# Gated linear attention and a gated SSM on one core: an opening in chunks, a later load of w_out, and other places for the steps of turns 1 to 5

## The chip, the core and the metric

The kernel runs on one core of a Trainium2 chip. The core has five engines with queues of their own, each of which works strictly in order: PE (TensorE, matrix products into PSUM), DVE (VectorE), ACT (ScalarE), POOL (GpSimd) and SP (SyncE, which here only issues DMAs). They meet through semaphores. The metric is the time of the whole program on the device in microseconds. A profiled execution gives, beside that time, the span and every instruction in it.

## The reference

Two blocks follow each other. All inputs are float32, save the weights of the second, which come as float64 and are cut to float32 bits on the chip.

```python
# attention: B, H, S, D = 4, 8, 768, 48; alpha lies between 0.8 and 1
for t in range(S):
    state = alpha[:, :, t, :, None] * state + einsum('bhd,bhe->bhde', k[:, :, t], v[:, :, t])
    y[:, :, t] = einsum('bhd,bhde->bhe', q[:, :, t], state)
x = y with the heads side by side                  # (4, 768, 384)
# gated SSM: w_in is 384 x 1024, w_out 512 x 384
val, gate = split(x @ w_in)
h = exp(A_log)[0] * h + val[:, t]                  # a scan over t, for 512 channels
out = (silu(gate) * h) @ w_out                     # (4, 768, 384)
```

## The kernel before

The sequence is cut into twelve turns of 256 steps, three to a batch element. A turn `m` passes through these stages, each a function of the program.

- Loads (`load_steps`, `load_raw`, `load_v`): alpha, q and k come with time over the partitions and must be turned so that the head's 48 channels lie over partitions. For turns 0 to 2 (and alpha of 3) PE turns them by products with the identity (`turned`) and ACT copies them out of PSUM; from turn 3 on DVE turns them with a stream transpose (`turn`). One buffer a name holds the raw steps, so a load waits until the turn before has been turned. Loads are issued by SP, one after the other.
- `scan_P` and `scan_V`: DVE's two scans of 1028 elements, the running product of alpha forwards and its sum backwards. `scaled_k` and `scaled_q` multiply k and q by them into `Zk` and `Zq`.
- `scores` (PE) and `masks` (DVE, ACT, POOL), together `first`: products of `Zk` and `Zq`, masked into `A` and `AK`. From turn 3 on the mask of `AK` is POOL's (line 762).
- `values(m, True)`, `states` and `add_up`, together `second`: masked scores times v, the states of four blocks of 64 steps, and their running sums `sum` on POOL (lines 828 and 830), or on DVE (`add_banks`) for the first batch element.
- `carried`, `values(m, False)` and `join`, together `third`: the part of the output that comes from earlier states, and the bringing of the two halves of y into `xT`, by ACT and by eight small DMAs.
- `project(n, cc)` for four pieces `cc`: 6 products with a piece of w_in, three for `val` and three for `gate`, then DVE's scan `hh` over `val` (line 932), ACT's `sg` = silu of `gate`, and their product, on DVE in the turns 0, 1 and 11 and on POOL in the others (line 942). `output(n)`: 8 products with w_out, ACT's eviction and the store.

The schedule is written out by hand: the order of the calls is the order of each engine's queue. Turn `n` of the loop projects turn `n` and does the attention of turn `m = n + 1`. DVE's seven steps for the turn after (turn alpha, scan P, turn k, scan V, `Zk`, turn q, `Zq`) are a generator, `products`, and `go(count)` takes the next `count` of its steps. Four PSUM banks (`ps_mm`) go round among turned pieces, scores, projections and outputs; the scores and y have four of their own.

w_in comes in pieces of 128 columns for each of `val` and `gate`. `low(i)` has ACT convert the low bits of piece `i`, `convert(i)` does the high bits on DVE (lines 553 and 555) and the sum on POOL (line 557); pieces 4 and 5 are w_out.

The opening, before the loop, is turn 0: turned alpha of turn 0 in four banks (line 694), q and k, alpha of turn 1, the scans, scores, masks, `first_values`, `states`, `first_states`, `first_carried` and `first_join`, with turning and converting for turn 1 in between. A memset of one element of the raw alpha by POOL (line 1001) holds back SP's loads behind it until w_in 0 is converted.

Of the kernel before, what the change touches and what calls it, by code (L numbers as in the profile page):

```python
# [346 lines left out]
def fast(  # L347
# [41 lines left out]
    p2 = pool("p2", 2)  # L389
    ps_at = pool("ps_at", 1, space=PS)  # L390
# [56 lines left out]
    units = [range(0, 1), range(1, 2), range(2, 4)]  # L447
# [45 lines left out]
    def constants():  # L493
# [18 lines left out]
        for t in dS[0] + dS[1]:  # L512
            nc.vector.memset(t[:, :, :, D:64], 0.0)
        for t in sums:
            nc.vector.memset(t[:, :, D:64], 0.0)
        nc.vector.memset(K0[:, :, :, D:], 0.0)
# [22 lines left out]
    def low(i):  # L539
        bits, w = bits_of(i)  # L540
        r = p2.tile([C, UW], I32, tag="wr", name="wr")
        lows[i] = r.rearrange("p (a n) -> p a n", a=w.shape[1])
        halves = lows[i].bitcast(U16).rearrange("p a (n two) -> p a n two", two=2)
        nc.scalar.activation(halves[:, :, :, 0], bits[:, :, :, 0], AF.Copy, scale=2.0 ** -29)

    def convert(i):
        if i not in lows:
            low(i)
        bits, w = bits_of(i)
        r = lows.pop(i)  # L550
        halves = r.bitcast(U16).rearrange("p a (n two) -> p a n two", two=2)
        quarters = bits.rearrange("p a n two -> p a (n two)").bitcast(U16).rearrange("p a (n four) -> p a n four", four=4)
        nc.vector.tensor_scalar(out=w.bitcast(U32), in0=bits[:, :, :, 1], scalar1=3, scalar2=0x3FFFFFFF,
                                op0=ALU.logical_shift_left, op1=ALU.bitwise_and)
        nc.vector.tensor_scalar(out=halves[:, :, :, 1], in0=quarters[:, :, :, 3], scalar1=0xC000, scalar2=None,  # L555
                                op0=ALU.bitwise_and)
        nc.gpsimd.tensor_tensor(out=w.bitcast(I32), in0=w.bitcast(I32), in1=r, op=ALU.add)  # L557
# [126 lines left out]
    def turned(m, name, js, t):  # L684
        raw = steps_of(name, m)
        tp = t[:, 0:len(js) * C].rearrange("p (j x) -> p j x", j=len(js))
        if (m, name) in ((1, "k"), (1, "q"), (3, "a")):
# [10 lines left out]
    def copy_turned(to, js, tp, engine=None):  # L698
        place = by_runs(to)[:, :, :, js.start:js.stop]
        if engine:  # L700
            return engine.tensor_copy(out=place, in_=tp)
        return nc.scalar.activation(place, tp, AF.Copy)

    def turn_over(m, name, to, tags=(None, None)):
        size = NJ // len(tags)
        copies = []
        for n, tag in enumerate(tags):
            js = range(size * n, size * (n + 1))
            copy = copy_turned(to, js, turned(m, name, js, bank(tag)), nc.vector if n % 2 and tag else None)
            if tag:  # L710
                for other in copies[(n + 1) % 2::2]:
                    tc.declare_no_dep(copy.ins, other.ins, reason="the copies write different steps")
                copies.append(copy)

    def alphas(m, tags=(None, None)):
        turn_over(m, "a", by_place(als[m % 2])[:, :, 1:GP], tags)
# [31 lines left out]
    def masks(m):  # L748
        sc = [[t[:, 0:4 * (L + D)].rearrange("p (h x) -> p h x", h=4) for t in pair] for pair in scs.pop(m)]
        mb = mask[:, None, :]  # L750
        if m < NG:
            for c in range(G):
# [162 lines left out]
    def project(n, cc, late=False):  # L915
# [10 lines left out]
        for vg, kk in order:  # L926
            nc.tensor.matmul((pv, pg)[vg], w_ins[cc][:, kk, vg, :], xT[:, kk, :],  # L927
                             start=(kk == 0), stop=(kk == NK - 1))
# [67 lines left out]
    for js, part in zip(halves, parts):  # L996
        copy_turned(tk, js, part)
# [230 lines left out]
```

## Time and profile before

| what | us |
|---|---|
| median of 3 runs | 278.73 (278.04 to 279.35) |
| the profiled execution | 279.43 |
| its span | 277.7 |
| PE busy in the span | 268.8 (97%) |
| DVE busy | 218.3 (79%) |
| POOL busy | 122.4 (44%) |
| ACT busy | 108.6 (39%) |
| first product with w_in starts at | 23.39 |

The clock that the throttle granted TensorE is 1.00 throughout. Times of the profile count from the start of the span. The chain that ended last lists, in order of time, the start of a piece, its length, and the engine, tile and line (or "issue", where an engine waited for nothing that the profile shows). A float32 product appears as two records. The instructions in order of time carry the start, the length, the engine, line and operation, output and input tiles, and in brackets the idle time just before and what ended it. A row of waits gives who waited, for whom, the sum, the count and the longest.

### The profile page before, as it was taken

The numbers are of one execution on the slowest core, as the hardware profiler recorded it, in microseconds if no ns is written. First come the engines' busy times: TensorE is split into PE (matmuls) and PEld (weight loads), VectorE is DVE, ScalarE is ACT, GpSimd is POOL, SyncE is SP. The second block draws the span as 40 slices with busy tenths as digits, with TensorE's granted clock in tenths as the row PEclk, the third lists the DMA queues.
The fourth block names the chain that finished last, engine by engine and source line by source line (L and its number), as shares of the span: only waits on it lengthen the run. The fifth ranks groups of instructions, "written<-read, shape, count | busy, mean of one in ns | idle before, by whom it ended". The sixth has DMA issues, their size and how long they took to land.

```text
span 277.7 us, 9598 instructions
## 1 busy us (share of the span) xinstructions
PE 268.8 (97%) x4056; PEld 217.0 (78%) x4056; DVE 218.3 (79%) x281; ACT 108.6 (39%) x244; POOL 122.4 (44%) x141
## 2 busy tenths in 40 slices
PE   7999999999989999899999999999999999999995
PEld 5988887876678688488688688688688688787874
DVE  7979998898798995995895995996995993079540
ACT  2577763461332532341542433433434425213111
POOL 8141223130068574563473584484384476435000
PEclk9999999999999999999999999999999999999999
DMA  6949993845919777487468587576687501201201
GB/s 196 295 140 309 296 262 78 205 88 139 267 48 238 149 199 182 103 214 163 103 181 199 114 205 164 130 197 155 152 186 159 144 0 27 77 1 33 71 5 59
DMA packets 51599, 41.18 MB, mean 148 GB/s; under 512 B 27360, under 2 KB 49536, under 8 KB 51552
## 3 DMA queue, kind: packets, MB, share of 16 engines
q1 hardware_dynamic: 48752, 37.50, 53.1%
q0 software_dynamic: 1408, 2.03, 2.8%
q10 hardware_dynamic: 1392, 0.99, 1.2%
q8 instruction: 33, 0.54, 0.9%
q14 instruction: 14, 0.11, 0.2%
HBM read 32.54 MB, written 4.72 MB: 134 GB/s over the span
## 4 chain that ended last, share of the span: by engine, by line
PE 92%; DVE 3%; DMA 1%; POOL 1%; issue 1%; ACT 1%; SPq 0%; DVEq 0%; ACTq 0%
PE mm L927 45%; PE mm L956 21%; PE y L791 4%; PE y L778 4%; PE mm L744 3%; PE s L744 3%; PE s L810 3%; PE mm L694 2%; PE mm L1189 2%; DMA raw_a<-in_alpha_dram 1%; POOL AK L762 1%; DVE P L630 1%; DVE V L649 1%; PE mm L689 1%; PE y L862 1%
## 5 line engine op out<-in xcount | busy, mean ns | idle before, releaser
L927 PE MATMUL mm<-xT,w_in 128*128 128x256 f32 x576 | 128.9, 382 | 0.6 <-ACT xT L884 0.6
L927 PEld LDWEIGHTS mm<-xT,w_in 128*128 128x128 f32 x576 | 108.1, 190 | 16.3 <-issue 0.8
L956 PE MATMUL mm<-w_out,f_last 128*128 128x384 f32 x160 | 54.1, 492 | 1.3 <-DVE A L759 1.3
L940 ACT ACTIVATE sg<-mm 128x256 f32<-128x256 f32 x48 | 18.4, 384 | 85.8 <-PE mm L927 80.3
L956 PEld LDWEIGHTS mm<-w_out,f_last 128*128 128x128 f32 x160 | 29.7, 190 | 21.1 <-issue 1.4
L830 POOL TENSOR_TENSOR sum<-sum,dS 128x192 f32<-128x192 f32 x30 | 33.2, 1108 | 27.3 <-PE mm L927 13.5
L942 POOL TENSOR_TENSOR f_last<-sg,hh 128x256 f32<-128x256 f32 x36 | 30.9, 862 | 30.6 <-ACT sg L940 23.1
L932 DVE TENSOR_TENSOR_SCAN hh<-a_dec,hh,mm 128x256 f32<-128x256 f32 x32 | 23.4, 732 | 15.4 <-PE mm L927 15.2
L630 DVE TENSOR_TENSOR_SCAN P<-al,lower 128x1028 f32<-128x1028 f32 x12 | 31.1, 2595 | 0.6
L649 DVE TENSOR_TENSOR_SCAN V<-al,ends 128x1028 f32<-128x1028 f32 x12 | 28.3, 2356 | 0.4
L907 POOL DMA_DIRECT2D xT<-yst x40 | 20.5, 517 | 13.1 <-ACT yst L904 11.8
L950 ACT ACTIVATE o_sb<-mm 128x384 f32<-128x384 f32 x22 | 10.8, 491 | 38.4 <-PE mm L956 38.4
L762 POOL TENSOR_TENSOR AK<-AK,mask 128x512 f32<-128x512 f32 x9 | 13.2, 1464 | 17.2 <-ACT AK L760 17.2
L759 DVE TENSOR_TENSOR A<-s,mask 128x256 f32<-128x256 f32 x9 | 3.8, 425 | 21.5 <-PE s L744 21.5
L557 POOL TENSOR_TENSOR w_in<-w_in,wr 128x768 int32<-128x768 int32 x4 | 7.3, 1826 | 26.0 <-DVE wr L555 17.0
L595 DVE STREAM_TRANSPOSE k<-raw_k 128x1024 f32<-128x1024 f32 x9 | 18.3, 2033 | 0.0
L595 DVE STREAM_TRANSPOSE q<-raw_q 128x1024 f32<-128x1024 f32 x9 | 18.2, 2022 | 0.0
L778 PEld LDWEIGHTS y<-AK,v 64*64 64x64 f32 x352 | 12.1, 134 | 6.4 <-issue 5.0
L595 DVE STREAM_TRANSPOSE al<-raw_a 128x1024 f32<-128x1024 f32 x8 | 16.3, 2041 | 0.1
L778 PE MATMUL y<-AK,v 64*64 64x64 f32 x352 | 14.5, 221 | 1.0 <-POOL AK L762 1.0
L791 PEld LDWEIGHTS y<-Zq,sum 48*64 48x64 f32 x656 | 11.8, 134 | 4.3 <-issue 4.1
L791 PE MATMUL y<-Zq,sum 48*64 48x64 f32 x656 | 14.4, 221 | 0.6 <-issue 0.6
(158 smaller groups left out, 392.2 us busy)
## 6 DMA issues: line engine op xcount, KB each, us to landing
v<-in_v_dram SPq DMA_DIRECT2D x22, 192.0 KB, 3.3
out_dram<-o_sb SPq DMA_DIRECT2D x22, 192.0 KB, 2.1
raw_k<-in_k_dram SPq DMA_DIRECT2D x18, 184.0 KB, 3.4
raw_q<-in_q_dram SPq DMA_DIRECT2D x18, 184.0 KB, 3.8
raw_k<-in_k_dram SPq DMA_DIRECT2D x18, 176.0 KB, 3.8
raw_q<-in_q_dram SPq DMA_DIRECT2D x18, 176.0 KB, 4.1
raw_a<-in_alpha_dram SPq DMA_DIRECT2D x16, 184.0 KB, 5.0
raw_a<-in_alpha_dram SPq DMA_DIRECT2D x16, 176.0 KB, 5.1
```

The costliest lines, as they stand in the source:

```text
L595: nc.vector.transpose(out=by_runs(to).rearrange("p h c j -> p h j c"), in_=raws[name][:, 0:4 * ROW].rearrange("p (h j d) -> p h j d", h=4, ...
L630: nc.vector.tensor_tensor_scan(out=P, data0=al[:, 0:4 * GP], data1=lower.rearrange("p h t -> p (h t)"), initial=0.0, op0=ALU.mult, op1=ALU ...
L649: nc.vector.tensor_tensor_scan(out=V[:, ::-1], data0=al[:, 1:4 * GP + 1][:, ::-1], data1=ends.rearrange("p h t -> p (h t)")[:, ::-1], init ...
L778: nc.tensor.matmul(ys[m][i][ds(64 * s, 64), e, ds(c * C + h * L, L)], v_sb[rows, c, 4 * i + p, :], As[i][rows, c, p, :], start=across and ...
L791: nc.tensor.matmul(ys[m][i][ds(64 * s, 64), e, ds(u * L, L)], Ss[j][rows, p, :], Zqs[m % 2][rows, u, p, D:], start=False, stop=True, skip_ ...
L830: nc.gpsimd.tensor_add(Ss[j][:, :, 0:D], Ss[j - 1][:, :, 0:D], part)
L907: engines[n % len(engines)].dma_start(out=xT[to, a], in_=st[rows, i, e])
L927: nc.tensor.matmul((pv, pg)[vg], w_ins[cc][:, kk, vg, :], xT[:, kk, :], start=(kk == 0), stop=(kk == NK - 1))
L932: nc.vector.tensor_tensor_scan(out=hh, data0=a_dec[:, cc:cc + 1].to_broadcast([C, GC]), data1=pv, initial=prev_h[cc][:, GC - 1:GC] if n % ...
L940: nc.scalar.activation(sg, pg, AF.Silu)
L942: f = lambda: engine.tensor_mul(fs[n][cc], sg, hh)
L956: nc.tensor.matmul(os[c], fs[n][cc][:, ds(c * C, C)], w_outs[cc // 2][:, cc % 2, :], start=(cc == 0), stop=(cc == NI - 1))
```

## The change

The opening works in smaller chunks: alpha of turn 0 is turned in quarters of 64 x 64 (`first_alphas`), q with its second half first (`first_q`), and k of turn 0 and alpha of turn 1 by transposes. The turned halves of k and q of turn 1 stand one by one between the scores, the states and the join. The masks of turn 0 come ahead of the conversion of w_in 0, and the conversion of w_in 1 moves behind the V scan of turn 1. Memsets of padding leave DVE: those of `dS` and `K0` fall away, those of `sums` are written by ACT. An ACT write after the first states takes the place of the memset that held back the loads.

In turn 0 the turning of alpha of turn 2 goes ahead of projection (0,1); the gate products of (0,0) and (0,1) go to turn 1, with four buffers for `sg`; values and states of turn 1 go between the two halves of projection (0,2). The load of w_out goes from the end of the opening to behind the third step of turn 1, and the load of k of turn 3 behind w_out. The last pieces of w_in are loaded one by one.

Later, `second(3)` and `second(5)` move behind the second projection of their turn, `first(5)` behind the output of turn 3, and `go` calls are moved so that three of DVE's steps for turn 6 fall into turn 3. The k of turn 4 is loaded behind the moves of the join, and the join of turn 2 uses both queues. From turn 5 on the order of PE, DVE, ACT and POOL is as before.

```diff
+    gates = pool("gates", 4)
...
-    units = [range(0, 1), range(1, 2), range(2, 4)]
+    units = [range(i, i + 1) for i in range(NI)]
...
-        for t in dS[0] + dS[1]:
-            nc.vector.memset(t[:, :, :, D:64], 0.0)
-        for t in sums:
-            nc.vector.memset(t[:, :, D:64], 0.0)
-        nc.vector.memset(K0[:, :, :, D:], 0.0)
...
     def convert(i):
         if i not in lows:
             low(i)
...
+        high(i)
+        add_low(i)
...
+    turned_by_transpose = ((0, "k"), (1, "a"), (1, "k"), (1, "q"), (3, "a"))
...
+    def first_alphas():
+        raw, to = steps_of("a", 0), by_runs(by_place(als[0])[:, :, 1:GP])
+        tps = [[bank(tag)[:, 0:NJ // 2 * 64].rearrange("p (j x) -> p j x", x=64) for tag in tags]
+               for tags in (("s0", "s1"), ("y1", "y0"))]
+        def turn_quarter(j, i, r):
+            rows = ds(64 * r, 64)
+            nc.tensor.matmul(tps[j // 4][r][ds(64 * i, 64), j % 4], raw[rows, ds(i * ROW + j * D, 64)],
+                             ident[rows, rows], start=True, stop=True, skip_group_check=True)
+        for j in range(2):
+            for r in range(2):
+                turn_quarter(j, 1, r)
+        for j in range(NJ):
+            for r in range(2):
+                turn_quarter(j, 0, r)
+                if j + 2 < NJ:
+                    turn_quarter(j + 2, 1, 1 - r)
...
+        for n in range(2):
+            for r in range(2):
+                place = to[:, :, ds(16 * r, 16), 4 * n:4 * n + 4]
+                part = tps[n][r].rearrange("p j (c h) -> p h c j", h=4)
+                copy = nc.vector.tensor_copy(out=place, in_=part) if r else \
+                    nc.scalar.activation(place, part, AF.Copy)
...
+    def first_q():
+        raw, to = steps_of("q", 0), plain("q")
+        tps = [bank().rearrange("p (j x) -> p j x", x=C) for _ in halves]
+        def turn_half(j, i):
+            nc.tensor.matmul(tps[j // 4][ds(64 * i, 64), j % 4], raw[:, ds(i * ROW + j * D, 64)], ident,
+                             start=True, stop=True, skip_group_check=True)
+        for j in range(4):
+            turn_half(j, 1)
+        for j in range(4):
+            turn_half(j, 0)
+            turn_half(4 + j, 1)
+        for j in range(4):
+            nc.tensor.transpose(tps[1][0:64, j], raw[:, ds((4 + j) * D, 64)], ident)
+        for js, part in zip(halves, tps):
+            copy_turned(to, js, part.rearrange("p j (c h) -> p h c j", h=4))
+        return to
...
-    def project(n, cc, late=False):
+    def project(n, cc, late=False, between=None):
...
+        passes(order[:NK] if between else order)
...
+        if between:
+            between()
+            passes(order[NK:])
+        sg = gates.tile([C, GC], FP32, tag="sg", name="sg")
         nc.scalar.activation(sg, pg, AF.Silu)
...
-    alphas(0, ("s0", "s1", "y1", "y0"))
-    tq = straighten(0, "q")
+    first_alphas()
+    for t in sums:
+        nc.scalar.activation(t[:, :, D:64], wide_S[0][:, 0:4 * (64 - D)].rearrange("p (j d) -> p j d", j=4), AF.Copy)
+    tq = first_q()
     tk = straighten(0, "k")
     alphas(1)
     P = scan_P(0)
+    last = P[:, :, GC]
+    nc.scalar.activation(ratio[:, 0], last, AF.Copy, scale=1.0 / FIRST_PRODUCT)
+    nc.scalar.activation(lower[:, :, 0], last, AF.Copy)
     V = scan_V(0, P, False)
-    halves = [range(0, NJ // 2), range(NJ // 2, NJ)]
-    parts = [turned(1, "k", js, bank()) for js in halves]
+    part = turned(1, "k", halves[0], bank())
     for c in range(G):
         scaled_k(0, tk, V, c)
         scaled_q(0, tq, P, c)
-    scores(0)
-    tk = plain("k")
-    for js, part in zip(halves, parts):
-        copy_turned(tk, js, part)
+    tk, tq = plain("k"), plain("q")
+    copy_turned(tk, halves[0], part)
+    for c in range(G):
+        scores(0, (c,))
+    part = turned(1, "k", halves[1], bank())
+    masks(0)
     low(0)
-    parts = [turned(1, "q", js, bank()) for js in halves]
-    convert(0)
-    nc.gpsimd.memset(raws["a"][0:1, 0:1], 0.0)
+    high(0)
+    add_low(0)
+    copy_turned(tk, halves[1], part)
+    first_values(True)
+    st = states(0)
+    part = turned(1, "q", halves[0], bank())
+    first_states(st)
+    copy_turned(tq, halves[0], part)
+    nc.scalar.activation(raws["a"][0:1, 0:1], sums[3][0:1, 0, 0:1], AF.Copy)
     load_steps("a", 2, [nc.sync])
     load_w(units[2], nc.sync)
-    masks(0)
-    low(1)
-    first_values(True)
-    st = states(0)
-    convert(1)
-    first_states(st)
-    tq = plain("q")
-    for js, part in zip(halves, parts):
-        copy_turned(tq, js, part)
-    last = P[:, :, GC]
-    nc.scalar.activation(ratio[:, 0], last, AF.Copy, scale=1.0 / FIRST_PRODUCT)
-    nc.scalar.activation(lower[:, :, 0], last, AF.Copy)
     for name in "kqa":
         load_steps(name, 2 + (name == "a"), [nc.sync])
+    load_w(units[3], nc.sync)
     load_v(1, nc.sync)
     P = scan_P(1)
     first_carried((1,))
     first_values(False)
     first_carried((2, 3))
+    part = turned(1, "q", halves[1], bank(), False)
     first_join()
+    low(1)
+    copy_turned(tq, halves[1], part)
     nc.scalar.activation(a_dec, a_log, AF.Exp)
     nc.scalar.activation(spare, minus, AF.Silu)
-    for half in range(2):
-        load_w_out(half, nc.sync)
     load_v(2, nc.sync)
     junk(0)
 
@@ -1044,40 +1098,42 @@
             carried(m, (1,))
             values(m, False)
             carried(m, (0, 2, 3))
-            join(m, [nc.sync] if m == 2 else [nc.sync, nc.gpsimd])
+            join(m, [nc.sync, nc.gpsimd])
             if m >= NG:
                 add_up(m, (3,))
 
+    late = (1, 3)
     for n in range(N):
         m = n + 1
         if n == 0:
             V = scan_V(1, P)
-            f0 = project(n, 0)
+            high(1)
+            fs_late = [project(n, 0)]
+            add_low(1)
+            alphas(2)
             scaled_k(1, tk, V)
             scaled_q(1, tq, P)
             low(2)
-            f1 = project(n, 1)
+            fs_late.append(project(n, 1))
             convert(2)
-            alphas(2)
-            low(3)
             first(m)
-            f0()
-            f1()
             tk = straighten(2, "k")
-            load_raw("k", 3, nc.sync)
             P = scan_P(2)
             tq = straighten(2, "q")
             V = scan_V(2, P)
+            low(3)
             convert(3)
             junk(1)
-            low(4)
-            f2 = project(n, 2)
-            values(m, True)
-            st = states(m)
-            add_banks(m, st)
+            def across_and_states():
+                values(m, True)
+                add_banks(m, states(m))
+
+            f2 = project(n, 2, between=across_and_states)
             alphas(3)
             third(m)
-            for name in "qa":
+            for half in range(2):
+                load_w_out(half, nc.sync)
+            for name in "kqa":
                 load_raw(name, 3 + (name == "a"), nc.sync)
             load_v(3, nc.sync)
             for c in range(G):
@@ -1093,6 +1149,8 @@
             values(m, True)
             st = states(m)
             add_banks(m, st)
+            for f in fs_late:
+                f()
             f3()
             f0 = project(n, 0)
             convert(4)
@@ -1103,8 +1161,8 @@
             f0()
             tk = plain("k")
             turn("k", tk)
+            third(m)
             load_raw("k", 4, nc.sync)
-            third(m)
             load_v(4, nc.sync)
             f1()
             junk(3)
@@ -1123,36 +1181,44 @@
         else:
             if n == 2:
                 first(m)
-                go(1)
-                f0 = project(n, 0)
-                second(m)
-                go(2)
-            else:
+            if n - 1 not in late:
                 second(m)
                 go(4)
-                f0 = project(n, 0)
+            else:
+                go(1)
+            f0 = project(n, 0)
             f0()
+            if n == 2:
+                go(2)
             load_raw("k", n + 3, nc.sync)
             load_raw("a", n + 3, nc.sync)
             go(1)
             f1 = project(n, 1)
             f1()
+            if n - 1 in late:
+                second(m)
+            if n == 4:
+                go(1)
             if n == N - 2:
                 for i in range(0, 2):
                     check_w(i)
             go(1)
             f2 = project(n, 2)
             f2()
-            load_raw("q", n + 3, nc.sync)
             if n == N - 2:
                 check_w(2)
             if n == N - 1:
                 check_flag()
-            go(1)
+            if n != 4:
+                go(1)
+            load_raw("q", n + 3, nc.sync)
             f3 = project(n, 3)
             f3()
             third(m)
-            first(m + 1)
+            if n not in late:
+                first(m + 1)
+            elif n > 2:
+                go(3)
             load_v(m + 2, nc.sync)
         if n == N - 2:
             for i in range(3, NW):
@@ -1163,6 +1229,8 @@
             value = nc.values_load(flag[0:1, 0:1], min_val=0, max_val=1)
         if 0 < n < N - 1:
             output(n)
+        if n > 1 and n in late:
+            first(m + 1)
     return value
```

72 lines of the change are left out of this document (35 added, 37 removed).

## The prediction

> **What bounds the kernel.** I read the page's busy shares first, then the waits of PE, then the busy time in stretches that follow the program's stages, and last the chain that ended last and each engine's instructions in order of time around the holes.
>
> ```profile
> PE 268.8 (97%) x4056; PEld 217.0 (78%) x4056; DVE 218.3 (79%) x281; ACT 108.6 (39%) x244; POOL 122.4 (44%) x141
> ```
> ```profile
> PE y L778 <- POOL AK L762: 1.0, 1, 1.0
> PE mm L956 <- DVE A L759: 1.3, 1, 1.3
> PE y L791 <- issue: 0.6, 1, 0.6
> ```
> ```profile
> 28.81:30.71 1.90, 1.90 (x36) 1.73 (x39) 1.90 (x4) 1.74 (x3) 0.00 (x0) 1.00 1.09 360
> 30.71:44.54 13.83, 13.18 (x357) 11.89 (x361) 12.79 (x22) 8.83 (x16) 3.66 (x2) 1.00 0.82 225
> ...
> 73.47:78.97 5.50, 4.49 (x78) 3.68 (x77) 4.18 (x5) 2.41 (x6) 3.03 (x1) 1.00 0.57 150
> ...
> 88.35:108.46 20.11, 20.11 (x308) 15.99 (x310) 17.75 (x17) 7.67 (x18) 12.76 (x14) 1.00 0.80 187
> 108.46:130.09 21.63, 20.38 (x309) 16.22 (x310) 17.35 (x17) 7.50 (x18) 10.43 (x13) 1.00 0.68 166
> ...
> 251.71:277.70 25.99, 22.77 (x187) 17.68 (x186) 12.11 (x29) 5.44 (x13) 2.78 (x5) 1.00 0.14 45
> ```
>
> Each row of the last view gives a stretch, its length and then PE's busy time. TensorE has work for 97% of the span. From 88.35 us on a turn costs about 20.1 us and PE is never idle in it (20.11 of 20.11), except for 1.25 us in the turn that begins at 108.46 (21.63 less 20.38) and 3.22 us at the very end, which the change does not touch. Ahead of that PE is idle 0.65 us in the second stretch and 1.01 us at the start of turn 2. So the change can win these three holes, 2.9 us in all, and whatever it takes off the opening, the 23.4 us before the first projection. The clock column is 1.00 in every stretch.
>
> The opening is a chain over the engines, here in order of time, with some later pieces that are used below:
>
> ```profile
> 4.79 1.56 PE s L694 x16
> 6.35 0.91 PE y L694 x16
> ...
> 7.87 2.31 DVE P L630
> ...
> 15.47 1.00 PE mm L744 x32
> ...
> 20.96 0.88 PE y L862 x42
> ...
> 21.90 0.98 PE y L870 x44
> ...
> 23.39 5.42 PE mm L927 x24
> ...
> 39.46 0.72 PE s L810 x64
> ...
> 44.54 0.76 PE s L744 x30
> ...
> 65.72 2.59 PE mm L927 x12
> ...
> 88.74 0.47 PE y L778 x32
> ...
> 112.81 5.40 PE mm L956 x16
> ```
> ```profile
> 17.20 0.42 DVE L754 TENSOR_TENSOR AK<-mm,mask 128x256 f32<-128x256 f32 x1
> ...
> 21.67 2.30 DVE L630 TENSOR_TENSOR_SCAN P<-al,lower 128x1028 f32<-128x1028 f32 x1
> ...
> 24.42 2.30 DVE L649 TENSOR_TENSOR_SCAN V<-al,ends 128x1028 f32<-128x1028 f32 x1
> ...
> 43.64 0.69 DVE L605 TENSOR_TENSOR Zq<-q,P 128x512 f32<-128x512 f32 x1
> ...
> 58.88 2.04 DVE L595 STREAM_TRANSPOSE k<-raw_k 128x1024 f32<-128x1024 f32 x1
> ```
> ```profile
> 19.90 0.33 ACT L877 ACTIVATE wide_S<-s 128x192 f32<-128x192 f32 x1 [0.30 <-PE s L810]
> ```
>
> **1. Alphas of turn 0 in quarters.** Now 32 records take 1.56 + 0.91 = 2.47 us, the first half 1.7 times as long as the second. New are 64 records over four quadrants of the array, 8 of them on the half that lands first. The nearest row is the values product, also 64x64 in four quadrants: 32 records in 0.47 us, so the other 56 cost 0.82 us at that pace and 1.4 us at 1.7 times it. I take 1.3 us, ending at 6.1 instead of 7.26, and with the memsets gone DVE is free for its copies. The first scan starts near 6.8 instead of 7.87: 1.1 us won. Bounds: 0.2 us (score records, 30 in 0.76 us, slowed 1.7 times) and 1.6 us (the values' pace).
>
> **2. The rest of the opening.** Scans and products keep their lengths, so the scores end at 16.47 - 1.1 = 15.4. The masks no longer stand behind a conversion of w_in; they end near 16.1, against 17.62. The turned pieces of q and the second of k come in chunks of 0.95 us (1.90 us for two, in the stretch at 28.81). PE's list: 15.4 + 0.95 (k) + 0.88 (values) + 0.72 (states) + 0.95 (q) = 18.9, where ACT has the first state done, then 0.5 (carried, half of 0.98) + 0.88 + 0.98 = 21.25, then 0.95 (q) while ACT copies xT. Projection (0,0) starts near 22.1 instead of 23.39: 1.3 us, bounds 0.4 and 2.0. The fills of `sums` go to ACT, between copies for which it waited: price 0.
>
> **3. The second piece of w_in goes behind the second V scan.** DVE now converts it only after `scan_V(1)`, POOL adds after that, and projection (0,1) needs the sum. The nearest rows are those of the third piece:
>
> ```profile
> 30.13 0.53 DVE L553 TENSOR_SCALAR w_in<-wbits 128x768 uint32<-128x768 uint32 x1
> 30.58 0.60 DVE L555 TENSOR_SCALAR wr<-wbits 128x768 uint16<-128x768 uint16 x1
> ...
> 31.33 1.84 POOL L557 TENSOR_TENSOR w_in<-w_in,wr 128x768 int32<-128x768 int32 x1 [9.58 <-DVE wr L555]
> ```
>
> From the start of the first to the end of the last are 3.04 us. The states end near 17.95 instead of 19.90, so the P scan starts 1.95 earlier, at 19.7, and V ends at 24.42 + 2.30 - 1.95 = 24.8; the weights are ready at 27.8. PE has done (0,0) and the alphas of turn 2 by 22.1 + 2.71 + 1.90 = 26.7 and waits 1.1 us, which eats most of part 2. Projection (0,1) ends at 30.5, and before the same work was done at 30.71. Net of parts 1 to 3: 0.2 us won. Bounds: 1.7 lost (no earlier P scan) and 1.3 won (no wait).
>
> **4. From there to turn 2.** The same PE work in another order, 13.18 us. DVE loses two gate products there; its last product before the scores of turn 2 ends at 44.33, the scores start at 44.54, so DVE keeps pace and PE bounds. The 0.65 us of "issue" lies inside a run of carried products; nothing in the change answers it: 0, between -0.65 and 0. The two gate products come back on DVE in turn 1, where PE waits for none of them: 0. The split load of w_in 2 and 3: 0, as more time is left for both.
>
> **5. Turn 2.** The values of turn 3 wait for POOL's mask:
>
> ```profile
> 75.88 3.03 POOL L762 TENSOR_TENSOR AK<-AK,mask 128x512 f32<-128x512 f32 x1 [17.21 <-ACT AK L760]
> 80.97 2.18 POOL L828 COPY sum<-dS 128x192 f32<-128x192 f32 x1 [2.06 <-ACT dS L818]
> 83.23 2.21 POOL L830 TENSOR_TENSOR sum<-sum,dS 128x192 f32<-128x192 f32 x2
> 85.40 1.43 POOL L942 TENSOR_TENSOR f_last<-sg,hh 128x256 f32<-128x256 f32 x2
> ...
> 93.24 1.26 POOL L762 TENSOR_TENSOR AK<-AK,mask 128x512 f32<-128x512 f32 x1
> ```
> ```profile
> 84.23 0.73 DVE L932 TENSOR_TENSOR_SCAN hh<-a_dec,hh,mm 128x256 f32<-128x256 f32 x1
> ```
>
> `second(3)` now stands behind two projections instead of one, 2.7 us later, and the mask is done by then: -1.0. This cover has a price of its own. Two gate products now go ahead of the sums on POOL, and the second needs hh of (2,1), which DVE delivers behind its Zk: at 84.96, now 84.75. Then 0.72 us for that product, and three sums; at the 0.72 of such a product each they end at 87.6. PE starts the third step near 88.35 - 0.2 - 1.0 = 87.15 and needs the last sum 1 us later. Price 0; upper bound 1.7, with the 4.39 us that the sums took in the rows above.
>
> **6. Turn 3.** `first(5)` goes behind the output, and with it go(3) puts two transposes and a P scan, 2.04 + 2.30 + 2.04 us, ahead of its masks. PE has the third step, the output (5.40) and the first scores to do meanwhile, so this is hidden. A wait of the output on these masks cannot occur in that order: -1.25, or 0 if something else made the hole.
>
> ```profile
> q14 instruction: 1, 0.01, 3.4%
> ```
>
> This row, from the DMA queues in the window 112 to 113, is the doubt: a packet of code moved while PE stood still. The Trainium skill, Runtime: NRT & Kernel Launch, section Instruction fetch mechanics, calls the crossing of a code block mostly hidden; by it the masks made the hole and the sum stays, and were it code the sum would be 1.25 us higher. No run here settles it yet.
>
> **7. Loads.** w_out goes behind the moves of xT of turn 1, and k, q and alpha of turn 3 behind w_out. The moves are split over SP and POOL in turn 1 too, and k of turn 4 goes behind them; xT of turn 2 is wanted only at 75. Price 0; see the slower rival.
>
> **Sum.** -0.2 - 1.0 - 1.25 = -2.45. The profiled execution took 279.43 us (span 277.7 and 1.73 around it), so 277.0; the median of the runs, 278.73, is 0.70 lower, and the forecast is 276.2.
>
> **Rivals.**
> *A, the opening keeps its gain.* If the weights come by 26.7, 1.3 us count in place of 0.2: 275.1, and with the 0.65 gone as well 274.5. For it: parts 1 and 2 are sums of short rows that I rounded up. Against it: two scans of 2.3 us follow each other on DVE and cannot begin before the first states.
> *B, no change.* POOL's sums are held up and the hole of turn 3 was not the masks: 276.2 + 1.7 + 1.25 = 279.2. For it: the copy of 2.18 us stood beside DVE work, and DVE's Zq falls into the new place of the sums. Against it: POOL's products took 0.72 beside DVE's transpose. The Trainium skill, SBUF — State Buffer, section Who interferes with whom, has a DVE instruction with two SBUF inputs and a POOL one that reads SBUF block each other whole; the 3.03 against 1.26 us of one mask agrees.
> *C, slower: k of turn 3 comes late behind w_out.*
>
> ```profile
> 45.19 3.15 SPq L907 DMA_DIRECT2D xT<-yst  x4
> ```
> ```profile
> wobits<-in_moe_w_out_dram SPq DMA_DIRECT2D x2, 768.0 KB, 7.4
> ```
>
> w_out is issued near 48.1 (48.34 less 0.2); at 7.4 us it lands by 56, and some 2 us sooner as its queue is then empty. Then 0.74 MB of k at 225 GB/s for a share of 0.82, so 274 GB/s, take 2.7 us: 56.7 to 58.7. DVE wants k at 58.7. Behind it stand the transpose, the V scan and the scan of (1,2), 2.04 + 2.30 + 0.73 and about 0.8 of small ones, whose bank projection (1,3) needs between 65.5 and 66.8. So PE waits only if k lands after about 60, and then us for us. Slower than before by over 1.4 us takes a landing past 64; at 65 the time is 281. For it: w_out and k now join q, alpha and v in the time that these three had. Against it: the margin.
>
> **Chances.** Forecast 0.50 (own range 275.2 to 277.3), A 0.13, B 0.20, C 0.12, and 0.05 for an opening that loses more than the rest wins. Under 0.5%, 1.4 us, a difference can about not be told from none. So faster 0.63, within 0.20, slower 0.17. The range, 274.3 to 279.3, leaves out C, the last case and the low end of A.
>
> **What would show it.** Right: the first P scan at 6.8, projection (0,0) near 22, a PE wait for POOL's w_in of about 1 us near 26.7, no PE wait for AK near 78 and none ahead of output 3, and turns of about 20.1 us from there on. Wrong: PE waiting for `sum` at the third step of turn 2, DVE idle on a DMA of raw_k or wobits between 52 and 62, or new "issue" holes in dense runs of small products.

## The result, and the profile after

The changed kernel takes 278.09 us (median of 22 runs, 276.77 to 281.62), the kernel before beside it 279.15 us (22 runs, 278.04 to 280.74). The ratio is 0.9964, 95% interval 0.9949 to 0.9979: about 1.0 us faster, under half of the 2.5 us forecast, and within 0.5% of no change. The range of the forecast holds the time; its likeliest case does not.

The profiled execution of the changed kernel was a good one: 277.4 us, span 275.7, 2.0 us under the profiled span of before. A second profile of the same kernel (`after_again`) has a span of 276.7, as the medians say. Both are read here. First the page's busy row, then the waits of PE, and PE's busy time in stretches; columns as in the prediction.

```profile
PE 269.3 (98%) x4060; PEld 216.1 (78%) x4060; DVE 217.9 (79%) x270; ACT 109.2 (40%) x251; POOL 121.2 (44%) x144
```
```profile
PE mm L974 <- ACT o_sb L1002: 1.2, 2, 1.0
```
```profile
29.97:42.94 12.97, 12.97 (x357) 11.76 (x360) 12.56 (x21) 7.80 (x15) 3.64 (x2) 1.00 0.50 126
66.50:89.94 23.44, 22.24 (x369) 17.27 (x368) 20.21 (x20) 7.63 (x19) 7.03 (x9) 1.00 0.87 212
```

The three waits of before (POOL's mask, the masks ahead of output 3, the 0.65 us of "issue") are gone: the first stretch of the view above is the counterpart of 30.71 to 44.54 of before, and PE is never idle in it. One wait is new: TensorE waits for ScalarE to evict output 1, and the stretch from output 1 to output 2 (the second row) takes 23.44 us. Before, and in the second profile, the stretches between outputs are these (from output 1 to 2, then from 2 to 4), first before, then `after_again`:

```profile
68.15:91.14 22.99, 21.98 (x370) 17.36 (x368) 19.83 (x20) 7.84 (x19) 11.55 (x9) 1.00 0.74 179
91.14:133.12 41.98, 40.73 (x629) 32.45 (x625) 34.24 (x32) 15.17 (x37) 22.38 (x27) 1.00 0.67 163
```
```profile
67.27:90.96 23.69, 22.25 (x370) 17.28 (x368) 20.00 (x20) 7.63 (x19) 7.01 (x9) 1.00 0.87 210
90.96:132.00 41.04, 41.04 (x628) 32.46 (x624) 34.67 (x32) 15.22 (x37) 24.32 (x27) 1.00 0.67 163
```

So against before the second profile has won 0.88 us by the start of output 1 (67.27 for 68.15), loses 0.70 in turn 2 and wins 0.94 in turns 3 and 4: 1.12 in all. The chain behind the loss stands in the rows of SyncE's queue and of ScalarE in the first profile:

```profile
46.19 1.10 SPq L460 DMA_DIRECT2D wobits<-in_moe_w_out_dram  x2
47.40 2.07 SPq L411 DMA_DIRECT2D raw_k<-in_k_dram  x4
49.57 5.86 SPq L411 DMA_DIRECT2D raw_q<-in_q_dram  x4
55.75 2.76 SPq L411 DMA_DIRECT2D raw_a<-in_alpha_dram  x4
59.02 1.37 SPq L441 DMA_DIRECT2D v<-in_v_dram  x2
60.52 5.84 SPq L953 DMA_DIRECT2D xT<-yst  x4
66.45 1.96 SPq L411 DMA_DIRECT2D raw_k<-in_k_dram  x4
68.51 1.14 SPq L441 DMA_DIRECT2D v<-in_v_dram  x2
69.75 2.88 SPq L1003 DMA_DIRECT2D out_dram<-o_sb  x2
```
```profile
SPq L411 <- DMA wobits<-in_moe_w_out_dram: 4.3, 2, 3.9
```
```profile
64.11 0.49 ACT L1002 ACTIVATE o_sb<-mm 128x384 f32<-128x384 f32 x1 [0.15 <-PE mm L1008]
...
73.99 0.49 ACT L1002 ACTIVATE o_sb<-mm 128x384 f32<-128x384 f32 x1 [6.91 <-DMA out_dram<-o_sb]
75.73 0.49 ACT L1002 ACTIVATE o_sb<-mm 128x384 f32<-128x384 f32 x1 [1.25 <-PE mm L974]
```

SyncE issues in order. Before it has issued q of turn 3 it waits 4.3 us for w_out to land, and everything behind is late. Nothing in q needs w_out. The operands of the issues in the trace show why it waits: SyncE's DMAs take eight completion semaphores in turn, and an issue first waits for the one that it will use. The two halves of w_out have numbers 107 and 108, and so have the third and fourth pieces of q, eight issues later; the fourth goes out only at 55.12. Output 0 is in SBUF at 64.6 (64.11 + 0.49), its stores start only at 69.75. There are two buffers for output rows, so ScalarE's first eviction of output 1 waits until the first store has landed, 73.99, and TensorE for the PSUM bank that it frees. Before, the stores were issued at much the same time, but the work was later, and nothing waited:

```profile
69.42 1.20 SPq L951 DMA_DIRECT2D out_dram<-o_sb  x2
```
```profile
72.92 0.49 ACT L950 ACTIVATE o_sb<-mm 128x384 f32<-128x384 f32 x1 [4.18 <-PE mm L956]
```

### The profile page after: what moved, and what is told of

Its sections match the earlier page's. It is cut to its first block, busy times and chain, and to the rows that moved or that the text cites. A ratio compares the mean times of both kernels' runs of the same rounds, so it can differ in the third digit from the quotient of the medians.

```text
span 275.7 us, 9644 instructions
## 1 busy us (share of the span) xinstructions
PE 269.3 (98%) x4060; PEld 216.1 (78%) x4060; DVE 217.9 (79%) x270; ACT 109.2 (40%) x251; POOL 121.2 (44%) x144
## 4 chain that ended last, share of the span: by engine, by line
PE 89%; DVE 4%; SPq 2%; DMA 1%; ACT 1%; issue 1%; DVEq 0%; ACTq 0%
PE mm L974 46%; PE mm L1008 19%; PE y L824 4%; PE y L837 4%; PE s L856 3%; PE mm L790 3%; PE s L790 3%; PE mm L700 2%; PE mm L1257 2%; DMA out_dram<-o_sb 1%; DVE V L653 1%; DVE P L634 1%; SPq L953 1%; PE mm L695 1%; PE y L908 1%
## 5 line engine op out<-in xcount | busy, mean ns | idle before, releaser
L994 POOL TENSOR_TENSOR f_last<-sg,hh 128x256 f32<-128x256 f32 x36 | 31.8, 887 | 33.1 <-ACT sg L992 20.3
L876 POOL TENSOR_TENSOR sum<-sum,dS 128x192 f32<-128x192 f32 x30 | 31.4, 1046 | 21.7 <-ACT dS L864 12.1
L953 POOL DMA_DIRECT2D xT<-yst x44 | 22.5, 517 | 12.8 <-ACT yst L950 12.8
L618 DVE TENSOR_TENSOR Zk<-k,V 128x1024 f32<-128x1024 f32 (+1 forms) x14 | 16.1, 1149 | 0.1
L609 DVE TENSOR_TENSOR Zq<-q,P 128x1024 f32<-128x1024 f32 (+1 forms) x14 | 14.8, 1060 | 0.1
```

What stands on the lines that cost most here:

```text
L876: nc.gpsimd.tensor_add(Ss[j][:, :, 0:D], Ss[j - 1][:, :, 0:D], part)
L953: engines[n % len(engines)].dma_start(out=xT[to, a], in_=st[rows, i, e])
L994: f = lambda: engine.tensor_mul(fs[n][cc], sg, hh)
```

## The experiments

### The changed kernel once more, and a third row buffer

> The changed kernel itself, on the chip of the next three. Theory S (the store wait): 0.8 to 1.3 us under the kernel before, ratio near 0.996, and in its profile ScalarE's evictions of output 1 wait 5 us or more for the stores of output 0, with TensorE waiting near 1.2 us for them. Rival R (the executions scatter and the profiled one was a good one): the same median, but the profile shows other waits than the first one, or this wait with a length that differs by over 1 us.

Measured: 278.27 us (before 279.30; ratio 0.9958, 0.9937 to 0.9979). The wait is the same one, ScalarE's evictions 6.9 and 1.5 us late, TensorE's 1.4 us. Theory S stands so far; most of what differs from the first profile lies ahead of turn 1 (see the last section).

```
-    rows = ctx.enter_context(tc.tile_pool(name="rows", bufs=2))
+    rows = ctx.enter_context(tc.tile_pool(name="rows", bufs=3))
```

> A third buffer for the rows of the output, so that the first eviction of output 1 needs no store of output 0 to land. Theory S: the 1.2 us that TensorE waits near 74 to 76 are gone, 1.2 us under the changed kernel, 2.2 us under the kernel before (ratio 0.992). Rival: another wait takes the time, the second eviction for the same stores or the mask of turn 3, and the time stays within 0.4 us of the changed kernel's.

Measured: 278.80 us (1.0002, 0.9975 to 1.0029), no gain. ScalarE in this run:

```profile
71.96 0.49 ACT L1002 ACTIVATE o_sb<-mm 128x384 f32<-128x384 f32 x1 [4.13 <-PE mm L1008]
76.75 0.49 ACT L1002 ACTIVATE o_sb<-mm 128x384 f32<-128x384 f32 x1 [4.30 <-DMA out_dram<-o_sb]
```

The first eviction no longer waits, the second still does, and runs at 76.75 as it did in `after_again`. Turn 2 takes 24.06 us. TensorE waits 1.9 us there; the profile names DVE's `hh`, which ended 0.34 us after that eviction, as the last releaser. The rival written for this run is what happened: one buffer more does not make stores land that were issued late.

### Which loads, and is it the loads or their order?

```
+    for half in range(2):            # opening, ahead of load_v(2)
+        load_w_out(half, nc.sync)
...
             tk = straighten(2, "k")
+            load_raw("k", 3, nc.sync)
...
-            for half in range(2):
-                load_w_out(half, nc.sync)
-            for name in "kqa":
+            for name in "qa":
```

> The changed kernel with w_out again issued in the opening and k of turn 3 again early in turn 0, as before; the rest as changed. Theory S: SyncE no longer waits 4.3 us for w_out to land before it issues q of turn 3, the stores of output 0 go out by 68 instead of 69.75, the wait near 74 to 76 shrinks to under 0.3 us: 1.0 to 1.3 us under the changed kernel. Rival (the loads cost nothing, as the prediction had it): within 0.3 us of the changed kernel.

Measured: 276.94 us (0.9917, 0.9886 to 0.9948), 1.33 us under `after_again`. Part 7 of the prediction had priced this at 0. The stores go out at 64.78, and from output 1 to output 2 it is 22.22 us, 1.47 less:

```profile
67.29:89.51 22.22, 22.14 (x369) 17.48 (x367) 19.83 (x20) 8.15 (x19) 8.49 (x9) 1.00 0.60 149
89.51:130.56 41.05, 41.05 (x629) 32.46 (x625) 35.16 (x32) 14.92 (x37) 24.68 (x27) 1.00 0.71 168
```

One load alone moved back, first k with w_out left late, then w_out with k left late:

> The changed kernel with k of turn 3 alone loaded early in turn 0 again; w_out stays late. Theory S1 (SyncE's wait of 4.3 us for w_out to land is what delays the stores): the wait stays, the stores of output 0 go out near 68, and turn 2 is 0.3 to 0.8 us shorter than the changed kernel's: 277.5 to 277.9. Rival S2 (the sum of both loads decides): without k's 2.1 us of issues the stores are in time and the time is 277.0.

> The changed kernel with w_out alone loaded in the opening again; k of turn 3 stays late. Theory S1: no wait of SyncE over 1 us between 47 and 56, the stores of output 0 go out before 68, no wait of TensorE near 75: 277.0, as with both loads early. Rival S2: half of the loss stays, 277.6. The prediction's rival C (k late for DVE): DVE idles for raw_k near 57 and the time is above 277.5.

Measured: 277.14 us (0.9914, 0.9897 to 0.9931) and 276.96 us (0.9900, 0.9883 to 0.9918). With k early SyncE still waits 3.3 us for w_out (now two pieces of alpha have its semaphores), but it has four issues fewer ahead, the stores go out at 66.85, and ScalarE evicts output 1 without that wait, as S2 had it. With w_out early the stores go out at 65.84 and that wait is gone too, as S1 had it; the 277.6 that S2 gave for this run did not come. So neither late load alone makes the stores too late: either load in its old place is enough.

The late loads kept, and only the order behind them changed:

```
             third(m)
-            load_raw("k", 4, nc.sync)
-            load_v(4, nc.sync)
             f1()
...
             output(0)
+            load_raw("k", 4, nc.sync)
+            load_v(4, nc.sync)
```

> The changed kernel with its late loads, but k and v of turn 4 are issued behind the stores of output 0 on SyncE's queue instead of ahead of them. Theory S (order on SyncE: the stores stand behind loads that wait for w_out): the stores go out near 67.5 instead of 70.4, output 1 is evicted without a wait of ScalarE over 1 us, TensorE's 1.0 to 1.4 us near 75 are gone, and turn 2 (from output 1 to output 2) takes 22.2 to 22.5 us instead of 23.4: 1.2 us under the changed kernel, 277.0. Rival D (the DMA engines themselves are behind, and the stores land late whatever their place): the wait stays over 0.7 us, the time within 0.4 us of 278.2.

Measured: 276.74 us (0.9899, 0.9882 to 0.9917), 2.8 us under the 279.54 of before beside it and the lowest median here, though not clear of `w_early` (0.9883 to 0.9918). Turn 2 takes 22.22 us, as with the loads early. SyncE still waits 3.6 us for w_out:

```profile
66.54 1.01 SPq L1003 DMA_DIRECT2D out_dram<-o_sb  x2
67.64 1.85 SPq L411 DMA_DIRECT2D raw_k<-in_k_dram  x4
```
```profile
72.01 0.49 ACT L1002 ACTIVATE o_sb<-mm 128x384 f32<-128x384 f32 x1 [4.18 <-PE mm L1008]
```

Rival D falls: with the stores out at 66.54 (70.41 in `after_again`) the wait is gone. What cost the change its gain was not that w_out came late for anyone who reads it, but what stood behind it.

### Turn 2: the values of turn 3 behind one projection again

```
             f0()
             if n == 2:
+                second(m)
                 go(2)
...
-            if n - 1 in late:
+            if n - 1 in late and n != 2:
                 second(m)
```

> The changed kernel with w_out and k of turn 3 loaded early, and the values and states of turn 3 again behind one projection of turn 2 instead of two. By the prediction's part 5 TensorE waits 1.0 us for POOL's mask again: 1.0 us above the same kernel without this edit (276.9), 277.9. Rival: the mask comes early enough in this order, since ScalarE copies AK sooner, and the time stays within 0.3 us of 276.9.

Both loads are early here, as in all runs whose names begin so. Measured: 277.87 us (0.9961, 0.9941 to 0.9981), 0.93 above `loads_early`. The wait is back, and turn 2 is as long as before:

```profile
PE y L824 <- POOL AK L808: 1.0, 1, 1.0
```
```profile
66.77:89.75 22.98, 21.98 (x369) 17.37 (x367) 19.81 (x20) 7.83 (x19) 11.54 (x9) 1.00 0.59 142
```

### Turn 3: masks or code?

```
-    late = (1, 3)
+    late = (1,)
...
-            if n == 4:
-                go(1)
...
-            if n != 4:
-                go(1)
+            go(1)
```

> The changed kernel with the scores of turn 5 and their masks again ahead of output 3, and the steps of turn 4 counted as before. Theory of the prediction, part 6: a hole of about 1.25 us is back ahead of output 3, and the time is 1.2 us above the changed kernel, about equal to the kernel before. Rival (a packet of code made the hole, or the cost only moved to the next turn): no hole, or a hole and a turn 4 that is shorter by as much; within 0.4 us of the changed kernel.

> The changed kernel with w_out and k of turn 3 loaded early, and the scores of turn 5 with their masks again ahead of output 3. Theory M: the hole of 1.25 us is back between the last score and output 3, 1.2 us above the same kernel without this edit (276.9), 278.1. Theory F: output 3 needs nothing of the masks; if there is a hole it lies inside the scores, ends 2.6 to 2.9 us after a packet of code, and the time is 276.9 to 278.2 by its length.

Measured: 279.39 us (1.0000, 0.9976 to 1.0023; the twelve executions run from 277.78 to 283.17), 1.1 above `after_again`; with the loads early 278.61 us (0.9991, 0.9967 to 1.0015), 1.7 above `loads_early`. The size looks like the prediction's part 6, but the hole is in another place. PE in `early_masks_first`:

```profile
108.19 0.95 PE L790 MATMUL s<-Zq,Zk 48*64 48x112 f32 x32
108.96 0.93 PE L790 MATMUL mm<-Zq,Zk 48*64 48x112 f32 x27
111.29 0.41 PE L790 MATMUL mm<-Zq,Zk 48*64 48x112 f32 x5 [1.40 <-issue]
111.64 0.59 PE L1008 MATMUL mm<-w_out,f_last 128*128 128x384 f32 x1
```

It lies between the 59th and the 60th record of the scores, which wait for no mask, and output 3 follows the last score at once. A packet of code starts 2.7 us before its end; this is the row of the window 108.5 to 108.6 of the DMA queues:

```profile
q8 instruction: 1, 0.02, 82.9%
```

That queue, q8, carries 33 such packets in the profiles of before, of the changed kernel and of the runs in the table below. The kernel before has one at 110.0 to 110.1, 2.8 us before the end of its hole at 112.81. Its row of the mask, read again, should have said so: the mask that was named as the releaser ended at 112.03 (111.61 + 0.42), 0.78 us before TensorE went on.

```profile
111.61 0.42 DVE L759 TENSOR_TENSOR A<-mm,mask 128x256 f32<-128x256 f32 x1 [0.34 <-PE mm L744]
```

To tell the two apart, TensorE's instruction stream was shifted by an edit to the warming products of the opening alone: they were cut smaller (42, then 66 records more), or one of them was replaced by small products (64 records more).

```
-    keep_warm(3, 256)
+    keep_warm(24, 32)                # before_shift42; (36, 8) in before_shift66
...
-    keep_warm(3, 256)
+    keep_warm(2, 256)                # the two runs with 64 more
+    t = bank("y0")
+    for n in range(33):
+        nc.tensor.matmul(t[0:64, 4 * n:4 * n + 4], wide_S[0][0:64, 0:64], wide_S[0][0:64, 0:4], ...)
```

> The kernel before, with its first six warming products of 256 columns cut into 48 of 32 columns: 42 more products ahead on TensorE's instruction stream, the same 2.9 us, and no other change. Theory M (the masks of turn 5 make the hole of 1.25 us ahead of output 3, as the prediction had it): the hole stays there with 1.25 us, and so does the wait of 1.0 us for POOL's mask in turn 2; the time stays within 0.4 us of the kernel before. Theory F (TensorE waits for its own next block of code, whose packet started 2.7 to 2.8 us before the end of the hole): the hole ahead of output 3 moves some 40 products forward, into the scores, or shrinks under 0.5 us, and the 0.65 us inside the carried products moves or goes; the wait for the mask stays at 1.0 us. Every hole with no releaser ends 2.6 to 2.9 us after the start of a packet of code on the queue that has 33 of them.

> As the last one, with 72 warming products of 8 columns: 66 more products ahead. Theory M: both holes where they were, 1.25 and 0.65 us, the time within 0.4 us of the kernel before but for the warming products. Theory F: the hole of turn 3 lies some 66 products earlier than before, at the end of the carried products or in the first scores, or it is gone; the time moves by the sum of the holes, by up to 1.9 us down.

> The kernel before with nothing but the 64 small products ahead, in place of one warming product. Theory F: the holes of 1.25 and 0.65 us are gone or moved, and unless others come up elsewhere the time from output 1 to output 4 falls from 64.97 to 63.7 us and the whole by 1.2 to 1.9 us less the small products' own time (up to 0.7): 277.4 to 278.6. Theory M: the wait ahead of output 3 stays at 1.25 us, 279.0 to 280.0. The wait of 1.0 us for POOL's mask stays in both.

> The kernel with both loads early and the scores of turn 5 ahead of output 3, whose hole was 1.4 us inside the scores (278.6 us against 276.9 with output 3 first), and with 64 more small products ahead on TensorE's instruction stream, in place of one of the three warming products. Theory F (code): the block's end lies elsewhere, the hole is gone or under 0.4 us, the two turns from output 2 to output 4 take 41.1 us instead of 42.5, and the time is 276.7 to 277.6, the small products costing up to 0.7 us. Theory M (the order of masks and output costs 1.25 us): the hole stays, 278.5 to 279.3.

In their times these four missed every forecast: 290.69, 291.88, 286.04 and 287.32 us (ratios 1.040, 1.046, 1.024 and 1.023; the last has six executions from 284.26 to 1586.51 us and allows no verdict). The warming products did not get shorter in proportion to their columns (6 records of 256 columns took 2.93 us, 48 of 32 columns 10.45 us, 66 of 4 columns in places of their own 7.20 us), so the turning of the first alphas began 6 to 12 us later, and the clock came up later too (see the last section). Later stretches can still be compared, and there the answer is clear. From output 1 to output 4 in `before_shift64`, and from output 2 to output 4 in `early_masks_first` and its shifted twin:

```profile
77.11:140.78 63.67, 62.66 (x993) 49.81 (x992) 54.06 (x52) 22.99 (x55) 35.60 (x35) 1.00 0.71 171
```
```profile
89.49:131.97 42.48, 41.08 (x628) 32.63 (x624) 34.08 (x32) 14.91 (x37) 23.58 (x27) 1.00 0.68 162
```
```profile
99.39:140.08 40.69, 40.69 (x626) 32.45 (x625) 33.79 (x31) 14.37 (x35) 22.73 (x25) 1.00 0.69 164
```

The first took 64.97 us before (22.99 + 41.98); the shift alone takes 1.30 off, and what is left idle is the 1.0 us for POOL's mask. The masks-first order without its hole is 40.69 us, even 0.36 less than output 3 first (41.05). New holes came elsewhere: in `before_shift42` one of 2.18 us in the scores at 203.74. Every hole of over 0.5 us without a releaser, in all these profiles:

| kernel | hole, us | its end | packet on q8 starts | end less start | product records before the end |
|---|---|---|---|---|---|
| before | 0.65 | 44.15 | 41.49 | 2.7 | 855 |
| before (named as a mask) | 1.25 | 112.81 | 110.02 | 2.8 | 1870 |
| masks_first | 1.32 | 110.67 | 108.09 | 2.6 | 1869 |
| early_masks_first | 1.40 | 111.29 | 108.59 | 2.7 | 1869 |
| before_shift42 | 1.81, 2.18, 0.71 | 31.84, 203.74, 245.34 | 29.41, 201.11, 242.84 | 2.4, 2.6, 2.5 | 475, 3136, 3768 |
| before_shift66 | 0.78 | 35.82 | 33.52 | 2.3 | 475 |
| before_shift64 | 1.28 | 30.89 | 28.45 | 2.4 | 475 |
| early_masks_first_shift | 2.14, 0.61 | 53.58, 99.11 | 50.99, 96.26 | 2.6, 2.8 | 982, 1616 |

Theory F stands, M falls. The last column, counted in the traces, is the strongest sign. With a spacing of 126.7 records, which is fitted to them, the eleven numbers leave remainders of 93.7 to 96.2 only, whatever product stands there and however many records were put ahead. The 4056 product records to the 33 packets of before give 123 to a packet, nearly the same spacing, so by this every hole lies at the same place of a block of code. What TensorE waits for at that place stays open in part. Each packet's own record ended 1.3 to 1.7 us before TensorE went on, and in six of the eleven holes before the hole began; that it is the late block is argued from the eleven intervals.

### The second piece of w_in ahead of the V scan again

```
-            V = scan_V(1, P)
             high(1)
+            V = scan_V(1, P)
```

> The changed kernel with both loads early, and the second piece of w_in converted ahead of the V scan of turn 1 again. The prediction's part 3: TensorE waits up to 1.1 us for this piece when it stands behind the scan, so the edit wins time, up to 1.1 us: 275.8 to 276.6. As the profile of the changed kernel has it, the piece is added 0.1 us before TensorE wants it, nothing is won, and V and the products of turn 1 behind it come 1.0 us later, up to 1.0 us of which the scores of turn 1 wait: 276.9 to 277.9.

Measured: 276.92 us (0.9911, 0.9889 to 0.9932), against 276.94: no difference. V of turn 1 starts 0.7 us later (23.19 for 22.50) and the scores of turn 1 where they did (30.62 for 30.64). What the later V loses, `Zk` wins back: it no longer stands beside POOL's sum and takes 1.19 us in place of 2.57, so `Zq` starts at 28.76 for 28.80.

## Why the prediction was wrong, step by step

**The step that failed: part 7, loads, "Price 0".** It asked when k, w_out and xT are wanted, and that part held: DVE began k of turn 3 at 58.39 (before 58.88), and rival C did not come. It did not ask what else stands on SyncE's queue. The stores of output 0 do, and in the kernel before they had just enough slack: issued at 69.42, with the eviction that needs their buffer at 72.92. Work that comes earlier by 1.65 us (the first profile), with the stores at 69.75, uses that slack up. Measured price: 1.47 us of turn 2 (23.69 against 22.22), 1.33 us of the time. Most of the rest of the miss of 1.9 us is that the 279.15 of 22 runs stand 0.42 above the 278.73 of three that the forecast went by; and 278.73 less 2.45 is 276.28, not 276.2. In rival C the prediction also let w_out land some 2 us sooner than the 7.4 us of before; its halves landed after 4.6 and 8.3 us.

**Parts 1 to 3** came out on both sides of the sum, 0.2. The scores of turn 1 start at 29.90 in the first profile and 30.68 in the second, 30.64 before: 0.74 or 0.0 won. The quarters started at 4.29, not at the 4.79 that the sum takes over from before, and their 1.3 us were 1.36 in the one and 2.25 in the other (the last section has the reason). The lower bound of part 1, 0.2 us won, is under 0.1 from its own rows. Projection (0,0) started at 22.37 and 23.03 for a forecast of 22.1. The wait of 1.1 us for the second piece of w_in did not occur. In the second profile the piece was ready at 27.84, as forecast (27.8), but TensorE came 1.2 us later than forecast, at 27.89. In the first, TensorE came at 27.11, and the P scan earlier than forecast, so the piece was ready at 27.07:

```profile
25.25 1.82 POOL L555 TENSOR_TENSOR w_in<-w_in,wr 128x768 int32<-128x768 int32 x1 [6.17 <-DVE wr L550]
```
```profile
27.11 2.86 PE L974 MATMUL mm<-xT,w_in 128*128 128x256 f32 x12
```

**Part 4, the "issue" hole, 0: wrong, and lucky.** The 0.65 us went in both profiles of the changed kernel, and in `before_shift64` by the shift alone. The prediction said that nothing in the change answers it. A change in the order or number of the products ahead can answer it, since it lies at the same place of a block of code as the other holes; in the two profiles of the changed kernel that place, 855 records in, comes 4.1 and 3.6 us after its packet's start, where it came 2.7 us after in before.

**Part 5 was right** in mechanism: the wait of 1.0 us went, and undoing the step brought 1.0 us of wait and 0.93 us of time back. Turn 2 without the store wait is 0.77 shorter than before, since TensorE is also busy 0.16 us longer (22.14 for 21.98). The sums on POOL were in time, as priced.

**Part 6: the size came, the mechanism was wrong.** Turns 3 and 4 are 0.94 shorter for a forecast of 1.25, but not because output 3 no longer waits for masks: it never did for most of that time. In the new order the same place of that block, 1869 records in, comes 6.0 us (`after_again`) after the packet's start, with output 3's slow products in between, and there is no hole; in `early_masks_first` it came 2.7 us after, 1.40 of it the hole. The doubt that the prediction put at the packet on q14 was right, with the wrong queue. The rule drawn on there, from the Trainium skill, Runtime: NRT & Kernel Launch, section Instruction fetch mechanics, calls the crossing of a code block mostly hidden. By count that agrees, two of 33 packets of before are followed by a hole; but these two were the two holes in question, and in the runs above such a crossing in or right behind a run of small products cost 0.6 to 2.2 us.

**The sum.** With the loads early the change is worth 0.86 us up to output 1 (67.29 for 68.15), 0.77 in turn 2 and 0.93 in turns 3 and 4: 2.56 (2.36 by the medians of the times), for a forecast of 2.45. That the two agree so well is partly chance: the 0.65 won without being forecast makes up for parts 5 and 6 being 0.55 smaller. As shipped, it is 0.88 - 0.70 + 0.94 = 1.12. Rival B gave the nearest time, 279.2, by other causes than the one that acted.

## What to carry to other kernels

When a load is moved on an in-order queue, list all that stands behind it to the end of the queue's slack, stores too: a store's buffer is someone's next output, and making the work earlier uses the same slack from the other side. An issue can also wait for a DMA that it does not need, here the one eight issues ahead. When a wait is named in a profile, compare the releaser's end with the waiter's start; 0.78 us between them meant that the named mask could not be the whole cause. A hole in a run of small products is worth testing by shifting the instruction stream, and by counting the records ahead of it, before any order is rewritten for it.

## What the runs showed of the hardware

TensorE stood still 0.6 to 2.2 us in or right behind dense runs of small products, eleven times at the same place of a block of some 127 product records, and each time went on 2.3 to 2.8 us after a packet of code had started (the table above).

The same opening ran in two paces. The 64 records of the quarters of the first alphas started at 4.29 in both profiles of the changed kernel, here the first, then `after_again`:

```profile
4.29 0.78 PE L716 MATMUL s<-ident,raw_a 64*64 64x64 f32 x29
...
4.97 0.68 PE L716 MATMUL y<-ident,raw_a 64*64 64x64 f32 x27
...
22.37 2.86 PE L974 MATMUL mm<-xT,w_in 128*128 128x256 f32 x12
```
```profile
4.29 1.19 PE L716 MATMUL s<-ident,raw_a 64*64 64x64 f32 x28
...
5.41 1.13 PE L716 MATMUL y<-ident,raw_a 64*64 64x64 f32 x28
```

They ended at 5.65 and 6.54, and the first P scan started at 6.38 and 7.16. Of the eleven profiles with this opening and the old warming products, three have that scan before 6.7 us and eight at 6.97 to 7.16. The clock column shows 1.00 in both, as it does for before, but it counts time for which the trace has no entry as full clock. The trace's list of clock periods begins, with the full clock, only 4.42 us after the start of the span in the first profile, at 7.19 in `after_again` and at 5.78 in before. In the three profiles with the early scan it begins at 4.42 to 5.00, in the eight others at 5.96 to 7.52. That the products are slower ahead of this entry shows best in `before_shift66`, where it stands at 20.40: the 16 records of `turned` that start at 18.66 took 1.90 us, and the 32 that start at 20.36 took 1.94.

The Trainium skill, TensorE: Matmul & The Clock Gate, section The HAM clock gate, says that the array starts at half its clock, that the window after which it is let up runs freely, and that the point therefore varies from run to run. The entries and the two paces agree with it.

The first P scan came 0.78 us apart in the two profiles of the changed kernel, and their spans are 1.0 us apart. So a single profiled pair (2.0 us) showed about twice what the medians show (1.06).

Warming records took 0.22 us each with 32 columns (48 in 10.45) as with 8 (72 in 15.53), and 0.11 us each with 4 columns and weights of half the width (66 in 7.20). Each record came with a weight load, of 128 columns in the first two and 64 in the last. That the loads set this pace is argued from the three rates and was not tested. In the four shifted kernels the first clock entry comes only at 14.47 to 20.40 us, so their openings also ran longer at the slower pace.
